# Attention backward: dK and dV products in bursts of two units instead of four, and operand loads cut into pieces on the queue of the crossbar transposes

## The chip, the core and the metric

The kernel runs on one core of one Trainium2 chip. The metric is the device time of one execution in microseconds. Three executions of the kernel before took 3423.2, 3423.9 and 3430.5 us; their median is 3423.9 us. One more execution was profiled: it took 3429.95 us, and its span from the first to the last instruction is 3427.8 us.

The engines are named as the profile names them: PE is the matrix engine (PEld its weight loads), DVE the vector engine, ACT the scalar engine with the exponential, POOL the GpSimd engine, SP the engine that issues most transfers. POOL and SP are used for transfers here: POOLq and SPq are the transfers that they issue.

## What is computed

The reference runs a transformer block with adaptive layer norms and takes its gradients for an output gradient. The change touches the backward pass of the attention alone: 32 heads of 16 columns over a sequence of 2048. Cut to that:

```python
q, k, v = (qkv[0], qkv[1], qkv[2])
scale = Dh ** (-0.5)
scores = jnp.einsum('bhqd,bhkd->bhqk', q, k) * scale
p = _softmax(scores, axis=-1)
o = jnp.einsum('bhqk,bhkd->bhqd', p, v)
...
_out, _vjp = jax.vjp(_f, A_x, A_wqkv, A_wo, B_w1, B_b1, B_w2, B_b2, c, w_mod)
_grads = _vjp(grad_out)
```

For each head the backward pass needs the probabilities again, the gradient of the scores from them and from dO times V, and then three products: dV from the probabilities and dO, dK from the score gradient and Q, dQ from the score gradient and K.

## The kernel before

The kernel is one program of several phases. The change lies in `attn_bwd`, which runs from about 1657 to 3251 us of the span.

**Tiling.** Heads go in quads `g` (8 of them), each in two pairs `jp` (16 pairs in all). For a pair the 2048 key columns go in 4 chunks `c` of 512, and for each chunk the 2048 query rows go in 16 tiles `ib` of 128. One pair of heads, one chunk and one row tile make a **unit** (1024 in all), and four units make a **group** (G = 4; 256 groups, 16 in a pair).

**One unit.** For each of its two heads `a`, PE computes a 128x512 tile of scores `st` (line 1198), ACT takes the exponential into one half of `pu` (line 1200), and PE computes a 128x512 tile of `dp`, dO times V (line 1201). The row sums that a softmax needs are folded into extra operand columns, so nothing else is done per element. Then DVE multiplies `dp` and `pu` into the unit's part of `ds` (line 1205). `st` has two buffers of one head, `dp` two of a unit: `dp` of a unit can't begin before DVE has read `dp` of the unit two before it, and `st` of a head can't begin before ACT has read `st` of the head two before it.

**dK and dV.** `kv` (line 1131) makes four products per unit, of 16 output rows by 512 columns each, into four bands of rows of one accumulator `acckv`, over the 16 row tiles of a chunk; the four run side by side on PE. They are collected in `pend` and run as **bursts**: `kv_group`, called after the second unit of a group, takes the four units of the group before it. After the last row tile of a chunk, DVE moves `acckv` into `kvT` (line 1134). After the last chunk of a pair, `turn` transposes `kvT` on PE in 16 steps (line 1140) into a buffer of `dp`, and ACT copies the result out (line 1144). `turn` runs ahead of the fourth unit of a group.

**dQ.** At the end of a group a crossbar transpose, issued by SP (line 1212), turns the 1 MB of `ds` into `dsT`. Its products `accq` (line 1151, eight per unit, 16 columns each) are laid between the matmuls of the units of the third group after it; DVE moves `accq` out once per pair (line 1158).

**Loads.** A quad needs `QT` and `dOT` (512 KB each) and `K`, `Q`, `dO` (256 KB each), in two buffers; `load_group` (lines 1117 and 1121) issues them on POOL at the start of the quad before. Each pair needs four masked operands, `KTm` and `VTm`, of 32 rows by 2048 columns; `load_masked` (line 462) issues them on POOL in pieces of 512 columns.

**Order.** PE runs in the order in which the code is written. The other engines' orders are made by a scheduler, within what the dependences allow. Each engine works through its own order strictly, so an instruction that waits holds up all behind it.

Of the kernel before, what the change touches and what calls it, by code (L numbers as in the profile page):

```python
# [8 lines left out]
BF16 = mybir.dt.bfloat16  # L9
# [9 lines left out]
P = 128  # L19
# [4 lines left out]
def chunks(total, size):  # L24
    out = []
    s = 0
    while s < total:
        w = min(size, total - s)
        out.append((s, w))
        s += w  # L30
    return out


class K:
# [219 lines left out]
    def phase12(self):  # L254
# [8 lines left out]
        with tc.tile_pool(name="p12", bufs=1) as sb, tc.tile_pool(name="p12e", bufs=8) as eb:  # L263
# [117 lines left out]
            with tc.tile_pool(name="p2c", bufs=1) as cp, tc.tile_pool(name="p2q", bufs=2) as qp, \  # L381
# [12 lines left out]
                for pidx in range(2 * NQ):  # L394
                    g, jp = divmod(pidx, 2)
                    heads = [4 * g + 2 * jp + a for a in range(2)]
                    if jp == 0:
                        T = self.load_quad(qp, srcs, g)
                    KT = T["KT"]
                    self.load_masked(masked, {"QT": (self.QTq_d, 0)}, g, jp)  # L400
# [679 lines left out]
    def attn_bwd(self):  # L1080
# [7 lines left out]
        tc, nc = self.tc, self.nc  # L1088
        S, D, H, NQ, ST, SC = self.S, self.D, self.H, self.NQ, self.ST, self.SC
        G = 4  # L1090
        W = 4 * DH
        with ExitStack() as es:
            qp = es.enter_context(tc.tile_pool(name="p5q", bufs=2))
            pup = es.enter_context(tc.tile_pool(name="p5pu", bufs=9))
            dsp = es.enter_context(tc.tile_pool(name="p5ds", bufs=3))
            dtp = es.enter_context(tc.tile_pool(name="p5dt", bufs=4))
            kvp = es.enter_context(tc.tile_pool(name="p5kv", bufs=1))
# [12 lines left out]
            masked = self.make_masked(cp, ["KT", "VT"])  # L1110
            pend, pendq = [], []

            def load_group(g):
                T = {}
                for n, src in fm.items():
                    t = qp.tile([P, S], BF16, name=f"{n}q")
                    nc.gpsimd.dma_start(t[:], src[g])
                    T[n] = t
                for n, src in tm.items():
                    t = qp.tile([P, ST, W], BF16, name=f"{n}g")  # L1120
                    nc.gpsimd.dma_start(t[:].rearrange("p st w -> p (st w)"), src[g])
                    T[n] = t
                return T

            def kv(u):
                (T, g, jp, c, ib, kvT, pu, ds) = u
                for j, (n, src) in enumerate((("Q", ds), ("dO", pu))):
                    for a in range(2):
                        r = 64 * j + 32 * a
                        col = (2 * jp + a) * DH  # L1130
                        nc.tensor.matmul(acckv[r:r + DH, :], lhsT=T[n][:, ib, col:col + DH], rhs=src[:, a, :],  # L1131
                                         start=(ib == 0), stop=(ib == ST - 1))
                if ib == ST - 1:
                    nc.vector.tensor_scalar(kvT[:, 512 * c:512 * (c + 1)], acckv[:], kvs[:], None, ALU.mult)

            def turn(g, jp, kvT):
                h0 = 4 * g + 2 * jp
                tp = dpp.tile([P, ST, P], BF16, name="dp")
                for st in range(ST):
                    nc.tensor.transpose(tp[:, st, :], kvT[:, st * P:(st + 1) * P], self.ident[:])  # L1140
                v = tp[:].rearrange("p s (t a e) -> p t s a e", t=2, a=2)
                for t, dst in enumerate((self.dk_t, self.dv_t)):
                    d = dst[:, :, h0 * DH:(h0 + 2) * DH].rearrange("p s (a d) -> p s a d", a=2)
                    nc.scalar.copy(d, v[:, t, :, :, 0:DH])

            def dq(u, heads):
                (T, g, jp, c, ib, i, dsT) = u
                for a in heads:
                    col = (2 * jp + a) * DH
                    for sub in range(4):  # L1150
                        nc.tensor.matmul(accq[:, ib, a, :], lhsT=dsT[:, (i * 2 + a) * 4 + sub, :],  # L1151
                                         rhs=T["K"][:, 4 * c + sub, col:col + DH],
                                         start=(c == 0 and ib == 0 and a == 0 and sub == 0), stop=False,
                                         skip_group_check=True)
                if c == SC - 1 and ib == ST - 1 and 1 in heads:
                    h0 = 4 * g + 2 * jp
                    d = self.dq_t[:, :, h0 * DH:(h0 + 2) * DH].rearrange("p s (a d) -> p s a d", a=2)
                    nc.vector.tensor_scalar(d, accq[:], self.scale, None, ALU.mult)

            def kv_group():  # L1160
                for u in pend[:G]:
                    kv(u)
                (T, g, jp, c, ib, kvT, pu, ds) = pend[G - 1]
                del pend[:G]
                return (g, jp, kvT) if c == SC - 1 and ib == ST - 1 else None

            msrc = {"KT": (self.KTq_d, 0), "VT": (self.VTq_d, 2)}
            self.load_masked(masked, msrc, 0, 0)
            T = load_group(0)
            turnq, hold = [], 0  # L1170
            with tc.manual_schedule(engines={mybir.EngineType.PE}):
                for g in range(NQ):
                    Tn = load_group(g + 1) if g + 1 < NQ else None
                    for jp in range(2):
                        if 2 * g + jp + 1 < 2 * NQ:
                            self.load_masked(masked, msrc, (2 * g + jp + 1) // 2, 1 - jp, eng=nc.gpsimd)
                        kvT = kvp.tile([P, S], BF16, name="kvT")
                        for c in range(SC):
                            c0 = 512 * c
                            for ib0 in range(0, ST, G):  # L1180
                                dsg = dsp.tile([P, G, 2, 512], BF16, name="ds")
                                for i in range(G):
                                    ib = ib0 + i
                                    q = slice(ib * P, (ib + 1) * P)
                                    uqs = []
                                    if len(pendq) > 2 * G:
                                        if pendq[0][3] == 0 and pendq[0][4] == 0 and hold:
                                            hold -= 1
                                        else:
                                            hold = 2 if pendq[0][4] else 0  # L1190
                                            uqs = [pendq.pop(0) for _ in range(2 if len(pendq) > 3 * G - i else 1)]
                                    if turnq and i == 3:
                                        turn(*turnq.pop(0))
                                    dp = dpp.tile([P, 2, 512], F32, name="dp")
                                    pu = pup.tile([P, 2, 512], BF16, name="pu")
                                    for a in range(2):
                                        stt = stp.tile([P, 512], F32, name="st")
                                        nc.tensor.matmul(stt[:], lhsT=T["QT"][:, q], rhs=masked["KT"][2 * jp + a][:, c0:c0 + 512],  # L1198
                                                         start=True, stop=True)
                                        nc.scalar.activation(pu[:, a, :], stt[:], ACT.Exp, scale=self.scale)  # L1200
                                        nc.tensor.matmul(dp[:, a, :], lhsT=T["dOT"][:, q], rhs=masked["VT"][2 * jp + a][:, c0:c0 + 512],  # L1201
                                                         start=True, stop=True)
                                        for uq in uqs:
                                            dq(uq, [a])
                                    nc.vector.tensor_tensor(dsg[:, i], dp[:], pu[:], ALU.mult)  # L1205
                                    pend.append((T, g, jp, c, ib, kvT, pu, dsg[:, i]))
                                    if i == 1 and len(pend) >= G + 2:
                                        r = kv_group()
                                        if r:
                                            turnq.append(r)  # L1210
                                dsT = dtp.tile([P, 8 * G, P], BF16, name="dsT")
                                nc.sync.dma_start_transpose(dsT[:], dsg[:].rearrange("p i a k -> p (i a k)"))
                                for i in range(G):
                                    pendq.append((T, g, jp, c, ib0 + i, i, dsT))
                    T = Tn
                turn(*kv_group())
                while pendq:
                    dq(pendq.pop(0), [0, 1])

# [263 lines left out]
```

## Time and profile before

| what | us |
|---|---|
| median of three executions | 3423.9 |
| the profiled execution | 3429.95 |
| its span | 3427.8 |
| PE busy in the span | 2957.0 (86%) |
| ACT busy | 2392.2 (70%) |
| DVE busy | 1877.4 (55%) |
| POOL busy | 372.7 (11%) |

The busy times are shares of a span with several phases, each with its own limit, so they don't tell what bounds the attention backward pass. PE busy counts pipelined matmuls by modelled ends: a PE that is shown as busy can still be waiting for its next operand. The DMA share counts the time of packets in flight on the core's 16 transfer engines; it goes over 1 where packets overlap. For a phase the useful views are the windows (busy time by stretch), the waits (who waited for whom) and the timeline (instructions in order, equal ones merged to a count, with the idle time before them and what ended it).

### The profile page before, as it was taken

The numbers are of one execution on the slowest core, as the hardware profiler recorded it, in microseconds if no ns is written. First come the engines' busy times: TensorE is split into PE (matmuls) and PEld (weight loads), VectorE is DVE, ScalarE is ACT, GpSimd is POOL, SyncE is SP. The second block draws the span as 40 slices with busy tenths as digits, with TensorE's granted clock in tenths as the row PEclk, the third lists the DMA queues.
The fourth block names the chain that finished last, engine by engine and source line by source line (L and its number), as shares of the span: only waits on it lengthen the run. The fifth ranks groups of instructions, "written<-read, shape, count | busy, mean of one in ns | idle before, by whom it ended". The sixth has DMA issues, their size and how long they took to land. (4 is left out here: it accounts for less than half of the span.)

```text
span 3427.8 us, 75641 instructions
## 1 busy us (share of the span) xinstructions
PE 2957.0 (86%) x31556; PEld 1444.9 (42%) x31556; DVE 1877.4 (55%) x2745; ACT 2392.2 (70%) x3577; POOL 372.7 (11%) x583
## 2 busy tenths in 40 slices
PE   5999998888884968578898998989999898999887
PEld 2455543333332433246444444444444444444433
DVE  6222220000004346545687887878788787888665
ACT  3899999999993324433576776777777777777633
POOL 3111210000002003330101010010101001000000
PEclk7999999999997989789999999999999999999998
DMA  3211110000004256564799999999999999999952
GB/s 116 68 50 49 45 46 11 6 12 12 6 1 153 96 175 216 118 204 140 156 181 184 182 188 182 180 189 179 192 183 187 186 178 194 179 179 176 188 172 66
DMA packets 1178339, 447.82 MB, mean 131 GB/s; under 512 B 1089162, under 2 KB 1145612, under 8 KB 1177996
## 3 DMA queue, kind: packets, MB, share of 16 engines
q1 hardware_dynamic: 1140188, 353.70, 53.4%
q0 software_dynamic: 29184, 79.59, 7.9%
q10 hardware_dynamic: 8624, 9.70, 0.9%
q8 instruction: 247, 4.05, 0.5%
q14 instruction: 96, 0.79, 0.1%
HBM read 106.83 MB, written 67.64 MB: 51 GB/s over the span
## 5 line engine op out<-in xcount | busy, mean ns | idle before, releaser
L1200 ACT ACTIVATE pu<-st 128x512 bf16<-128x512 f32 x2048 | 1143.5, 597 | 411.1 <-PE st L1198 404.3
L1205 DVE TENSOR_TENSOR ds<-dp,pu 128x1024 bf16<-128x1024 f32 x1024 | 1212.5, 1220 | 323.8 <-ACT pu L1200 306.4
L413 ACT ACTIVATE pu<-st 128x1024 bf16<-128x1024 f32 x1024 | 940.1, 1376 | 4.7 <-PE accbank L419 4.7
L1201 PE MATMUL dp<-VTm,dOTq 128*128 128x512 bf16 x2048 | 778.1, 380 | 102.9 <-DVE ds L1205 101.3
L1198 PE MATMUL st<-KTm,QTq 128*128 128x512 bf16 x2048 | 778.8, 380 | 8.2 <-DMA dOTq<-dOTq_d 7.6
L1151 PEld LDWEIGHTS <-dsT 128*128 128x128 bf16 x8192 | 488.4, 96 | 650.9 <-issue 203.1
L410 PE MATMUL st<-QTm,KTq 128*128 128x512 bf16 x2048 | 607.0, 377 | 7.0 <-ACT pu L413 1.5
L1151 PE MATMUL accq<-Kg,dsT 128*128 128x16 bf16 x8192 | 493.6, 170 | 33.0 <-DMA dsT<-ds 33.0
L419 PEld LDWEIGHTS <-pu 128*128 128x128 bf16 x8192 | 291.2, 96 | 458.7 <-ACT pu L413 408.2
L419 PE MATMUL accbank<-Vaug,pu 128*128 128x17 bf16 x8192 | 353.4, 172 | 67.6 <-DVE accbank L406 7.4
L428 DVE RECIPROCAL rl<-accbank 128x4 f32<-128x4 f32 x128 | 23.0, 180 | 526.0 <-PE accbank L419 525.6
L1131 PE MATMUL acckv<-ds,Qg 128*16 128x512 bf16 x2048 | 267.0, 382 | 0.8 <-DVE ds L1205 0.7
L1131 PE MATMUL acckv<-pu,dOg 128*16 128x512 bf16 x2048 | 267.0, 382 | 0.0
L1198 PEld LDWEIGHTS <-QTq 128*128 128x128 bf16 x2048 | 196.0, 96 | 134.5 <-issue 131.2
L1201 PEld LDWEIGHTS <-dOTq 128*128 128x128 bf16 x2048 | 196.8, 96 | 27.9 <-DVE ds L1205 18.7
L462 POOL DMA_DIRECT2D KTm<-KTq_d x120 | 60.0, 500 | 1121.3 <-PE dp L1201 1037.0
L288 DVE TENSOR_SCALAR ev_fm<-pps,bcol 128x512 bf16<-128x512 f32 x92 | 69.1, 751 | 195.5 <-PE pps L281 194.6
L410 PEld LDWEIGHTS <-KTq 128*128 128x128 bf16 x2048 | 129.6, 96 | 35.5 <-issue 20.5
L281 PE MATMUL pps<-xhat1T,wpad 128*128 128x512 bf16 x384 | 122.8, 378 | 4.9 <-DVE ev_fm L288 3.8
L1131 PEld LDWEIGHTS <-Qg 128*16 128x16 bf16 x2048 | 74.4, 88 | 74.7 <-issue 10.7
L549 ACT ACTIVATE rT<-ups,bias 128x512 bf16<-128x512 f32 x56 | 38.5, 688 | 52.1 <-PE ups L547 52.0
L1131 PEld LDWEIGHTS <-dOg 128*16 128x16 bf16 x2048 | 74.2, 88 | 0.0
(304 smaller groups left out, 2383.1 us busy)
## 6 DMA issues: line engine op xcount, KB each, us to landing
rT_d<-rT SPq DMA_DIRECT2D x4, 1792.0 KB
rT<-rT_d SPq DMA_DIRECT2D x4, 1792.0 KB
duT_d<-duT POOLq DMA_DIRECT2D x4, 1792.0 KB, 12.7
rT_f<-rT_d SPq DMA_DIRECT2D x14, 512.0 KB
duT_f<-duT_d POOLq DMA_DIRECT2D x14, 512.0 KB, 3.9
xhat_d<-xhat SPq DMA_DIRECT2D x2, 2048.0 KB
QTq_d<-ev_fm POOLq DMA_DIRECT2D x32, 128.0 KB, 2.1
QTm<-QTq_d SPq DMA_DIRECT2D x128, 32.0 KB
```

What stands on the lines that cost most here:

```text
L281: nc.tensor.matmul(pt[:, :sw], lhsT=wpads[t][:, kt, g, :], rhs=xhat1T[:, kt, s0:s0 + sw], start=(kt == 0), stop=(kt == DT - 1))
L288: nc.vector.tensor_scalar(ev[:, :sw], pt[:, :sw], bc, None, ALU.add)
L410: nc.tensor.matmul(stt[:, a, :qw], lhsT=KT[:, kb * P:(kb + 1) * P], rhs=QTm[a][:, q0:q0 + qw], start=True, stop=True)
L413: nc.scalar.activation(pu[:, :, :qw], stt[:, :, :qw], ACT.Exp, scale=self.scale)
L419: nc.tensor.matmul(acc[:, a, sub, :], lhsT=pu[:, a, sub * P:(sub + 1) * P], rhs=Vaug[:, kb, heads[a], :], start=False, stop=False, skip_gr ...
L462: eng.dma_start(masked[n][j][r:r + 32, c0:c0 + cw], src[g, r:r + 32, c0:c0 + cw])
L1131: nc.tensor.matmul(acckv[r:r + DH, :], lhsT=T[n][:, ib, col:col + DH], rhs=src[:, a, :], start=(ib == 0), stop=(ib == ST - 1))
L1151: nc.tensor.matmul(accq[:, ib, a, :], lhsT=dsT[:, (i * 2 + a) * 4 + sub, :], rhs=T["K"][:, 4 * c + sub, col:col + DH], start=(c == 0 and i ...
L1198: nc.tensor.matmul(stt[:], lhsT=T["QT"][:, q], rhs=masked["KT"][2 * jp + a][:, c0:c0 + 512], start=True, stop=True)
L1200: nc.scalar.activation(pu[:, a, :], stt[:], ACT.Exp, scale=self.scale)
L1201: nc.tensor.matmul(dp[:, a, :], lhsT=T["dOT"][:, q], rhs=masked["VT"][2 * jp + a][:, c0:c0 + 512], start=True, stop=True)
L1205: nc.vector.tensor_tensor(dsg[:, i], dp[:], pu[:], ALU.mult)
```

## The change

`kv_group` becomes `kv_two`: it runs two units and is called after the second and after the fourth unit of a group, whenever four units are pending. `turn` moves from ahead of the fourth unit to ahead of the third. `pu` gets 6 buffers instead of 9. `load_group` only makes a list of pieces: `QT` and `dOT` in two halves of 256 KB, `K`, `Q` and `dO` whole. `pair_pieces` lists the four masked operands of a pair in pieces of 32 rows by 2048 columns. The main loop issues one piece on SP ahead of a group, and all loads leave POOL.

```diff
-            pup = es.enter_context(tc.tile_pool(name="p5pu", bufs=9))
+            pup = es.enter_context(tc.tile_pool(name="p5pu", bufs=6))
...
             def load_group(g):
-                T = {}
+
+                T, pieces = {}, []
                 for n, src in fm.items():
-                    t = qp.tile([P, S], BF16, name=f"{n}q")
-                    nc.gpsimd.dma_start(t[:], src[g])
-                    T[n] = t
+                    t = T[n] = qp.tile([P, S], BF16, name=f"{n}q")
+                    for (s0, sw) in chunks(S, 1024):
+                        pieces.append((t[:, s0:s0 + sw], src[g, :, s0:s0 + sw]))
                 for n, src in tm.items():
-                    t = qp.tile([P, ST, W], BF16, name=f"{n}g")
-                    nc.gpsimd.dma_start(t[:].rearrange("p st w -> p (st w)"), src[g])
-                    T[n] = t
-                return T
+                    t = T[n] = qp.tile([P, ST, W], BF16, name=f"{n}g")
+                    pieces.append((t[:].rearrange("p st w -> p (st w)"), src[g]))
+                return T, pieces
+
+            def pair_pieces(g, jp):
+                pieces = []
+                for n, src, sh in (("KT", self.KTq_d, 0), ("VT", self.VTq_d, 2)):
+                    for j in (2 * jp, 2 * jp + 1):
+                        r = 32 * ((j + sh) % 4)
+                        pieces.append((masked[n][j][r:r + 32, :], src[g, r:r + 32, :]))
+                return pieces
...
-            def kv_group():
-                for u in pend[:G]:
+            def kv_two():
+                for u in pend[:2]:
                     kv(u)
-                (T, g, jp, c, ib, kvT, pu, ds) = pend[G - 1]
-                del pend[:G]
+                (T, g, jp, c, ib, kvT, pu, ds) = pend[1]
+                del pend[:2]
                 return (g, jp, kvT) if c == SC - 1 and ib == ST - 1 else None
...
-                    Tn = load_group(g + 1) if g + 1 < NQ else None
                     for jp in range(2):
-                        if 2 * g + jp + 1 < 2 * NQ:
-                            self.load_masked(masked, msrc, (2 * g + jp + 1) // 2, 1 - jp, eng=nc.gpsimd)
+                        pieces = []
+                        if jp == 0:
+                            pieces = pair_pieces(g, 1)
+                        elif g + 1 < NQ:
+                            Tn, pieces = load_group(g + 1)
+                            pieces = pair_pieces(g + 1, 0) + pieces
...
+                                if pieces and (c or ib0):
+                                    nc.sync.dma_start(*pieces.pop(0))
...
-                                    if turnq and i == 3:
+                                    if turnq and i == 2:
                                         turn(*turnq.pop(0))
...
-                                    if i == 1 and len(pend) >= G + 2:
-                                        r = kv_group()
+                                    if i % 2 == 1 and len(pend) >= 4:
+                                        r = kv_two()
```

**What PE runs around `turn`.** The first place is the start of the second pair of heads on PE. The rows are instructions in PE's order; `...` stands for rows that repeat these and for the dQ products. Before, the burst (here its last product) is followed by the two heads of the third unit, and only then come the transposes of `kvT` and the fourth unit:

```order
L1131 MATMUL acckv<-pu,dOg 16x512
L1198 LDWEIGHTS QTq
L1198 MATMUL st<-KTm_20941,QTq 128x512
...
L1201 MATMUL dp<-VTm_20949,dOTq 128x512
...
L1198 MATMUL st<-KTm_20943,QTq 128x512
...
L1140 LDWEIGHTS kvT
L1140 MATMUL dp<-ident,kvT 128x128
```

At the same place the change has, after the end of the burst, the transposes at once and then the third unit:

```order
L1139 MATMUL acckv<-pu,dOg 16x512
L1148 LDWEIGHTS kvT
L1148 MATMUL dp<-ident,kvT 128x128
...
L1211 LDWEIGHTS QTq
L1211 MATMUL st<-KTm_20941,QTq 128x512
...
L1214 MATMUL dp<-VTm_20949,dOTq 128x512
```

So the unit that stood between the burst and `turn` is gone from there. DVE's order of `ds` and `kvT` is the same before and after: the move of `acckv` stands behind the `ds` of the unit that precedes the burst.

**What SP runs around the start of a quad.** Before, SP has nothing but the 256 transposes in this phase. With the change its order around the start of the second quad is the following (`x15` counts equal rows; `KTm_20945` and `_20947` are the masked operands of the next pair but one half, `QTq` to `dOg` those of the quad after):

```order
L1225 DMA_TRANSPOSE dsT<-ds 128x32x128 x15
L1193 DMA KTm_20945<-KTq_d 32x2048
L1193 DMA KTm_20947<-KTq_d 32x2048
L1225 DMA_TRANSPOSE dsT<-ds 128x32x128
L1193 DMA VTm_20953<-VTq_d 32x2048
L1193 DMA VTm_20955<-VTq_d 32x2048
L1193 DMA QTq<-QTq_d 128x1024
L1225 DMA_TRANSPOSE dsT<-ds 128x32x128
L1193 DMA QTq<-QTq_d 128x1024
L1193 DMA dOTq<-dOTq_d 128x1024
L1225 DMA_TRANSPOSE dsT<-ds 128x32x128
L1193 DMA dOTq<-dOTq_d 128x1024
```

Behind these stand `Kg` and `Qg`, a transpose, `dOg`, and twelve transposes more. The scheduler has not kept one piece per group: eleven pieces stand among five transposes, up to three in a row, at the start of a quad; at the start of a quad's second pair four pieces stand around one transpose.

More of the change, by code (lines that the diff above doesn't have):

```diff
@@ L1158, in dq @@
                     nc.vector.tensor_scalar(d, accq[:], self.scale, None, ALU.mult)
-            def kv_group():
-                for u in pend[:G]:
+            def kv_two():
+                for u in pend[:2]:
                     kv(u)
-                (T, g, jp, c, ib, kvT, pu, ds) = pend[G - 1]
-                del pend[:G]
+                (T, g, jp, c, ib, kvT, pu, ds) = pend[1]
+                del pend[:2]
                 return (g, jp, kvT) if c == SC - 1 and ib == ST - 1 else None
-            msrc = {"KT": (self.KTq_d, 0), "VT": (self.VTq_d, 2)}
-            self.load_masked(masked, msrc, 0, 0)
-            T = load_group(0)
+            T, pieces = load_group(0)
+            for (d, sr) in pair_pieces(0, 0) + pieces:
+                nc.sync.dma_start(d, sr)
             turnq, hold = [], 0
@@ L1215, in attn_bwd @@
                     T = Tn
-                turn(*kv_group())
+                turn(*kv_two())
                 while pendq:
```

## The prediction

> **What bounds the kernel now.** I read the windows first, for the stretch in which the changed code runs, then the waits in it, then the timeline of one group. The columns of a window are its length, the busy time of PE, PEld, DVE, ACT and POOL with counts, the granted PE clock, the DMA share and GB/s.
>
> ```profile
> 1659.00:3240.00 1581.00, 1449.52 (x16556) 708.59 (x16556) 1262.98 (x1106) 1157.64 (x2079) 127.44 (x255) 0.99 1.04 183
> ```
>
> The phase takes 1581 us, 46% of the span. PE is busy for 92% of it, DVE for 80%, ACT for 73%: no engine is full, so the loop between them must set the pace. The waits of this stretch (who waited for whom, us in total, times, longest) say where:
>
> ```profile
> ACT pu L1200 <- PE st L1198: 404.3, 525, 7.7
> DVE ds L1205 <- ACT pu L1200: 306.4, 502, 7.5
> PE dp L1201 <- DVE ds L1205: 101.3, 271, 0.7
> PEld L1151 <- DMA dsT<-ds: 34.1, 7, 7.8
> ```
>
> ACT waits for PE, DVE for ACT and PE for DVE, some 500 times or two per group of 256: a ring. Apart from it, PE's weight loads waited 34.1 us for a late transpose, in 7 pieces of up to 7.8 us. The timeline of one group (start us, length, engine, line, count, idle time before) shows the ring turning:
>
> ```profile
> 2301.52 0.38 PE L1198 MATMUL st<-KTm,QTq 128*128 128x512 bf16 x1
> 2302.12 0.39 PE L1131 MATMUL acckv<-ds,Qg 128*16 128x512 bf16 x2
> 2302.78 0.38 PE L1131 MATMUL acckv<-ds,Qg 128*16 128x512 bf16 x2
> 2303.10 0.39 PE L1198 MATMUL st<-KTm,QTq 128*128 128x512 bf16 x1
> 2303.53 2.73 ACT L1200 ACTIVATE pu<-st 128x512 bf16<-128x512 f32 x5 [0.99 <-PE st L1198]
> 2303.64 0.38 PE L1198 MATMUL st<-KTm,QTq 128*128 128x512 bf16 x1
> 2304.69 2.36 DVE L1205 TENSOR_TENSOR ds<-dp,pu 128x1024 bf16<-128x1024 f32 x2 [0.90 <-ACT pu L1200]
> 2305.24 0.38 PE L1198 MATMUL st<-KTm,QTq 128*128 128x512 bf16 x1
> 2305.97 0.38 PE L1201 MATMUL dp<-VTm,dOTq 128*128 128x512 bf16 x1 [0.35 <-DVE ds L1205]
> 2306.28 0.38 PE L1198 MATMUL st<-KTm,QTq 128*128 128x512 bf16 x1
> 2306.81 0.38 PE L1198 MATMUL st<-KTm,QTq 128*128 128x512 bf16 x1
> 2307.09 0.38 PE L1201 MATMUL dp<-VTm,dOTq 128*128 128x512 bf16 x1
> 2307.41 0.38 PE L1198 MATMUL st<-KTm,QTq 128*128 128x512 bf16 x1
> 2308.02 0.39 PE L1131 MATMUL acckv<-ds,Qg 128*16 128x512 bf16 x2
> ```
>
> From burst to burst (2302.12 to 2308.02) a group takes 5.90 us. One head takes 0.535 us (2303.10 to 2303.64 and on to 2305.24, four heads), eight of them 4.28. The burst of four rounds holds PE from 2302.12 to 2303.10, 0.98 us, and begins 0.065 us later than a head would have (2301.52 + 0.535). Its rounds start 0.22 us apart (2302.12 to 2302.78 in three steps), so 0.88 is work and 0.165 its two edges. That makes 5.33; the other 0.57 is waiting: `st` at 2305.24 is followed at 2306.28 (1.04, so 0.505 too much) and 2306.81 at 2307.41 (0.065). During a burst nothing new reaches ACT, so DVE starts late afterwards (2304.69, after 0.90 idle), and the third unit behind the burst finds `dp` occupied.
>
> **The change, part by part.**
>
> *Two bursts of two units.* Each costs two rounds and two edges, 0.44 + 0.165 = 0.605 us; two of them and eight heads make 4.28 + 1.21 = 5.49. Does the wait go? Two units and a burst last 4 x 0.535 + 0.605 = 2.745 us. Counted from the first `st` behind a burst (2303.10), the next-but-one unit's `dp` would come at 2.745 + 0.22 (one matmul) = 2.965, one unit later 4.035. DVE released them at 2305.97 and 2307.09, 2.87 and 3.99 behind that `st`. Both are in time, by 0.095 and 0.045 us; DVE then has its next unit only 2.745 us after the last start, against 2 x 1.14 of work (2.36 for two in the row, whose last lasts 1.22). So the wait goes, narrowly: 5.90 - 5.49 = 0.41 per group, 256 x 0.41 = **105 us** gained. I take the margins as they stand; if they fail by 0.05 us it is 512 x 0.05 = 26 less.
>
> The Trainium skill, "TensorEngine Tiling (Array Packing)", section "Key Properties", says that a change of the tiling mode drains PE; it speaks against twice as many bursts, and the edges agree with it. By it the edges' 0.165 x 256 = 42 us is the price, which stands in the sum above already; without it the gain would be 147.
>
> *The move of `acckv` into `kvT`.* These rows are DVE's moves and ACT's copies:
>
> ```profile
> L1134 DVE TENSOR_SCALAR kvT<-acckv,kvs 128x512 bf16<-128x512 f32 x64 | 47.5, 742 | 0.5 <-PE acckv L1131 0.5
> L1158 DVE TENSOR_SCALAR dq_t<-accq 128x512 bf16<-128x512 f32 x15 | 10.2, 680 | 0.0
> ```
>
> Before, DVE's idle 0.90 us covered the 0.74. Afterwards DVE has 2.745 - 2.28 = 0.465 idle per two units, so each of the 48 moves that isn't ahead of a `turn` pushes DVE back by about 0.28, of which the margins take 0.1: 0.18 x 48 = **9 us** lost (bounds 0 and 48 x 0.74 = 36). The 15 moves of `accq` meet the same lack of cover: 16 x 0.2 = **3 us**.
>
> *`turn` directly behind the burst.* Before, around a `turn`:
>
> ```profile
> 2355.15 0.39 PE L1131 MATMUL acckv<-ds,Qg 128*16 128x512 bf16 x2
> 2356.12 0.39 PE L1198 MATMUL st<-KTm,QTq 128*128 128x512 bf16 x1
> 2356.73 0.74 DVE L1134 TENSOR_SCALAR kvT<-acckv,kvs 128x512 bf16<-128x512 f32 x1
> 2357.20 1.05 PE L1140 MATMUL dp<-ident,kvT 128*128 128x128 bf16 x16
> 2358.29 0.59 ACT L1144 COPY dk_t<-dp 128x512 bf16<-128x512 bf16 x1 [0.61 <-PE dp L1140]
> 2359.25 2.74 ACT L1200 ACTIVATE pu<-st 128x512 bf16<-128x512 f32 x5
> 2362.59 0.39 PE L1131 MATMUL acckv<-ds,Qg 128*16 128x512 bf16 x2
> ```
>
> That group took 7.44 us, 1.54 over a usual one: about the 1.05 of the transposes and a wait of half a microsecond. The unit between burst and `turn` (2356.12 to 2357.20) covered DVE's move. With the change nothing stands there. The `ds` ahead of the move ends 3.99 - 2.745 = 1.2 us after the burst, the move about 1.9, so the last four transposes wait and end near 2.25 (their first twelve read older chunks). ACT's two copies then hold it for 0.96 (2358.29 to 2359.25), so the third unit's first exponential starts near 3.4 instead of 2.25 + 0.43, and with two buffers of `st` the fourth unit waits the 0.7 out. So `turn` costs 2.25 + 0.7 = 2.95 in place of 1.54: 16 x 1.4 = **22 us** lost. Bounds: 0 if the copies find cover, 16 x 2.5 = 40 if both waits are felt in full twice.
>
> *Loads on SP.* SP's own instructions, and the two transposes around a load of quad operands beside a usual one:
>
> ```profile
> L1212 SPq DMA_TRANSPOSE dsT<-ds x256: 4766/5049/16257, 1665.1 to 3238.1; - x128
> L462 SPq DMA_DIRECT2D KTm<-KTq_d x8: 313/417/553, 1485.3 to 1489.9; - x8
> 2251.92 13.19 SPq L1212 DMA_TRANSPOSE dsT<-ds  x1
> 2301.18 4.79 SPq L1212 DMA_TRANSPOSE dsT<-ds  x1
> QTq<-QTq_d POOLq DMA_DIRECT2D x8, 512.0 KB, 5.1
> dOTq<-dOTq_d POOLq DMA_DIRECT2D x8, 512.0 KB, 6.6
> 2265.00:2271.00 6.00, 2.29 (x17) 1.03 (x18) 1.18 (x2) 1.19 (x2) 0.00 (x0) 0.82 1.24 215
> ```
>
> The transpose that meets POOL's load takes 13.19 us instead of 4.79, and soon after (2265 to 2271) PE is busy for 2.29 of 6 us at a clock of 0.82. This is where the 34.1 us of the waits come from. On SP the pieces stand in line with the transposes. For SP, a quad is 32 transposes of 5.05 (median) and 15 pieces of 0.42, 168 us, against at least 32 x 5.49 = 176 for PE: SP keeps up, by 5%. Locally, eleven pieces in five transposes add 4.6 us, while five groups leave 5 x (5.49 - 5.05) = 2.2 and the `turn` among them 2.95; and a transpose 8.4 us late cost a wait of at most 7.8, of 4.9 on average (34.1 / 7), so some 3.5 us of lateness aren't felt. I expect the load stalls to go but for **5 us**, a gain of 29; the bounds are 0 and 34 left. POOL's issues wait on nothing of the path, so their going gains nothing. Six buffers of `pu` cover four pending units and two in progress: no cost.
>
> *Sum*, against the profiled execution of 3429.95 us (its span 3427.8, about 2 us around it): 105 - 9 - 3 - 22 + 29 = 100 us gained, 3330. The profiled execution lies 6 us above the median of the three runs, so against that: 3423.9 - 100 = 3324 us.
>
> **The rivals.**
>
> *A: the load stall stays.* The same 2.25 MB must pass within five transposes; in line ahead of a transpose they delay it as they did beside it. For it: SP is left only 5%. Against it: the pieces are spread over some 28 us, where POOL issued all in about 5. All 34 stay: 3324 + 29 = 3353. The Trainium skill, "DMA: Bandwidth & Descriptors", section "Issuing engines are not separate DMA queues", would give this: transfers of all issuers run on the same engines, and the issuer changes only the time of issuing. No run here shows it for one queue yet.
>
> *B: the ring stays tight.* The margins of 0.095 and 0.045 us are small, and a burst of two rounds may have dearer edges than a quarter of a long one shows. At 0.05 per two units: 3324 + 26 = 3350.
>
> *C: the change doesn't do what it says.* DVE still holds PE up for the whole 0.57 per group, because a burst of any length empties ACT. Then the edges add 42, the moves and `turn` 34, the loads give 29: 47 us slower, 3471. Against it: the release times above.
>
> *D: ordinary transfers and transposes drain each other in one queue.* A quad has seven places where SP goes from transposes to pieces and back. If each costs D, SP needs 168 + 7D per quad. Today's pace is 1581 / 8 = 197.6 us, so it decides against the change from D = 4.2 us on; at the 6.6 us that a quad's `dOTq` took to land it is 214 per quad, 8 x 16.6 = 133 us slower, 3557 from the median. For it: landings of 5.1 and 6.6 us are of that size. Against it: POOL's pieces of `KTm` flowed beside transposes in every pair without lengthening a group.
>
> **Chances.** Forecast 0.62, A 0.16, B 0.14, C 0.03, D 0.05. The predicted time is that of the forecast. Its own range is 3308 (no load stall left, `turn` covered by half) to 3340; A and B reach to 3353 and, with each other in part, 3365. I give 3308 to 3365, which leaves out C, D and A with B in full. A measurement can tell about 0.2% (7 us) from no change: faster 0.91 (forecast, A, B less a remainder in which they add up), same 0.02, slower 0.07.
>
> **What the profile afterwards would show.** Right: bursts 2.75 us apart, the waits of `dp` for `ds` far under 101 us, PE busy near 98% between loads; after each pair one gap of 2 to 3 us with PE's transposes waiting for `kvT`; no transpose over 7 us, no PE wait for `dsT` over 2 us. A shows as waits for `dsT` of 4 to 8 us at the quads' starts; B as many waits of `dp` under 0.1 us; C as bursts 2.95 us apart; D as transposes or gaps of SP of 5 us and more around each piece. The forecast is wrong if two bursts and two pairs of units take more than 5.6 us, or if SP, never idle, sets the pace.

## The result, and the profile after

The changed kernel takes 3329.6 us (median of four runs, 3329.1 to 3331.1) against 3427.2 us (3423.2 to 3431.3) of the kernel before in the same runs: a ratio of 0.9716 [0.9699, 0.9733], faster. The profiled executions took 3329.45 and 3429.95 us: 100.5 us gained, and the account below is made between these two. Between the medians it is 97.7 us, and 3329.6 lies 5.6 us above the forecast of 3324, which was worked out from 3423.9 us before.

The windows view of the changed kernel over the stretch of the attention backward pass (columns as in the prediction):

```profile
1656.00:3150.00 1494.00, 1450.57 (x16611) 702.85 (x16609) 1257.00 (x1113) 1149.57 (x2083) 1.50 (x2) 1.00 1.08 196
```

The two windows leave out the ends of the phase, so their lengths aren't the gain: from its first `st` to its last move of `accq` the phase lasts 1500.2 us, and 1595.1 before. The PE work in it is the same: PE is now busy for 97% of the window, not 92%. POOL's 127 us of work have gone. The waits of this stretch, for the changed kernel (who waited for whom, us in total, times, longest):

```profile
ACT pu L1213 <- PE st L1211: 298.1, 527, 2.1
DVE ds L1218 <- ACT pu L1213: 226.9, 451, 5.0
...
PEld L1148 <- DVE kvT L1142: 17.3, 16, 1.1
...
PE dp L1148 <- DVE kvT L1142: 14.4, 15, 1.0
PEld L1159 <- DMA dsT<-ds: 13.6, 12, 2.4
...
PE accq L1159 <- DMA dsT<-ds: 7.7, 8, 1.9
PE dp L1214 <- DVE ds L1218: 5.8, 15, 0.4
```

The third link of the ring is open: `dp` waited 101.3 us in 271 pieces for `ds`, and now 5.8 us in 15. ACT and DVE still wait for what is ahead of them, but PE hardly waits for `ds` any more. Two larger waits of PE are left: sixteen times for `kvT`, once per pair, which is new, and twelve times for a transpose, 13.6 us instead of 34.1. Its timeline over one group (start us, length, engine, line, count, idle time before):

```profile
2300.25 0.39 PE L1139 MATMUL acckv<-ds,Qg 128*16 128x512 bf16 x2
2300.47 0.38 PE L1139 MATMUL acckv<-ds,Qg 128*16 128x512 bf16 x2
2300.80 0.39 PE L1211 MATMUL st<-KTm,QTq 128*128 128x512 bf16 x1
...
2301.34 0.38 PE L1211 MATMUL st<-KTm,QTq 128*128 128x512 bf16 x1
...
2302.38 2.35 DVE L1218 TENSOR_TENSOR ds<-dp,pu 128x1024 bf16<-128x1024 f32 x2 [0.40 <-ACT pu L1213]
...
2303.01 0.39 PE L1139 MATMUL acckv<-ds,Qg 128*16 128x512 bf16 x2
...
2305.77 0.39 PE L1139 MATMUL acckv<-ds,Qg 128*16 128x512 bf16 x2
```

The bursts start at 2300.25, 2303.01 and 2305.77: 2.76 us for two units, 5.52 for a group, in place of 5.90. Heads follow each other after 0.54 us and no `dp` waits. DVE idles 0.40 us per two units.

The timeline around a `turn` of the changed kernel:

```profile
2212.57 0.39 PE L1139 MATMUL acckv<-ds,Qg 128*16 128x512 bf16 x2
...
2213.22 0.83 PE L1148 MATMUL dp<-ident,kvT 128*128 128x128 bf16 x12
...
2214.21 0.74 DVE L1142 TENSOR_SCALAR kvT<-acckv,kvs 128x512 bf16<-128x512 f32 x1
...
2215.01 0.40 PE L1148 MATMUL dp<-ident,kvT 128*128 128x128 bf16 x4 [0.96 <-DVE kvT L1142]
...
2215.45 0.58 ACT L1152 COPY dk_t<-dp 128x512 bf16<-128x512 bf16 x1 [2.47 <-PE dp L1148]
...
2216.40 2.21 ACT L1213 ACTIVATE pu<-st 128x512 bf16<-128x512 f32 x4
...
2217.07 0.38 PE L1211 MATMUL st<-KTm,QTq 128*128 128x512 bf16 x1 [0.61 <-ACT pu L1213]
...
2218.21 0.39 PE L1139 MATMUL acckv<-ds,Qg 128*16 128x512 bf16 x2
```

From burst to burst 5.64 us instead of 2.76: a `turn` costs 2.88 us. Twelve transposes read older chunks; the last four wait 0.96 us for DVE's move, and a later `st` waits 0.61 us for ACT, which the copies had held.

Last, SP's own timeline at the start of a quad, and its transposes as a group (number: shortest, median, longest in ns), both of the changed kernel:

```profile
1838.61 5.18 SPq L1225 DMA_TRANSPOSE dsT<-ds  x1
1843.83 1.04 SPq L1193 DMA_DIRECT2D VTm<-VTq_d  x2
1844.92 1.33 SPq L1193 DMA_DIRECT2D QTq<-QTq_d  x1
1846.36 5.30 SPq L1225 DMA_TRANSPOSE dsT<-ds  x1
1851.70 0.57 SPq L1193 DMA_DIRECT2D QTq<-QTq_d  x1
1852.32 0.43 SPq L1193 DMA_DIRECT2D dOTq<-dOTq_d  x1
1852.85 5.87 SPq L1225 DMA_TRANSPOSE dsT<-ds  x1
1858.76 0.57 SPq L1193 DMA_DIRECT2D dOTq<-dOTq_d  x1
```

```profile
L1225 SPq DMA_TRANSPOSE dsT<-ds x256: 4699/5106/6867, 1662.8 to 3141.0; - x128
```

The longest transpose is 6.9 us, where those beside POOL's loads of a quad had taken 12 to 16. The scheduler lays one to three pieces between two transposes, not one as the code is written. For a while SP falls behind PE: from 1838.61 to the transpose at 1846.36 it takes 7.75 us, and PE's group 5.52.

### The profile page after: what moved, and what is told of

It reads as the page before. It is cut to its first block, busy times and chain, and to the rows that moved or that the text cites. A ratio compares the mean times of both kernels' runs of the same rounds, so it can differ in the third digit from the quotient of the medians.

```text
span 3327.6 us, 75207 instructions
## 1 busy us (share of the span) xinstructions
PE 2954.7 (89%) x31556; PEld 1438.8 (43%) x31556; DVE 1866.0 (56%) x2745; ACT 2381.2 (72%) x3577; POOL 231.7 (7%) x303
## 5 line engine op out<-in xcount | busy, mean ns | idle before, releaser
L1139 PE MATMUL acckv<-ds,Qg 128*16 128x512 bf16 x2048 | 309.1, 382 | 0.8 <-DVE ds L1218 0.7
L1139 PE MATMUL acckv<-pu,dOg 128*16 128x512 bf16 x2048 | 309.1, 382 | 0.0
L652 PE MATMUL daps<-gT,W2gbT 128*128 128x512 bf16 x224 | 58.5, 404 | 19.3 <-DVE duT L654 19.3
L725 ACT COPY a_blk<-trps 128x1024 bf16<-128x1024 bf16 x28 | 28.3, 1012 | 59.0 <-PE trps L722 58.9
```

Source lines behind the costliest of these rows:

```text
L652: nc.tensor.matmul(pt[:, :sw], lhsT=W2gbT[:, kt, ft * P:(ft + 1) * P], rhs=gT[:, kt, s0:s0 + sw], start=(kt == 0), stop=(kt == DT - 1))
```

## The experiments

Each kernel is the changed one with the edit shown (cut to its main lines), timed beside the kernel before on the chip that it ran on (about 3433 us there); ratios are to that.

**One part of the change at a time.** First, bursts of two, but the loads back on POOL, whole and at the places that they had before:

```diff
-    nc.sync.dma_start(*pieces.pop(0))
+    Tn = load_group(g + 1) if g + 1 < NQ else None
...
+    self.load_masked(masked, msrc, (2 * g + jp + 1) // 2, 1 - jp, eng=nc.gpsimd)
```

> The change's bursts, place of turn and buffers of pu, with the loads as before on POOL. Theory (the loads on SP gave back 26 us): the load stalls of about 38 us return, the time is 3330 + 26 = 3356 us, one transpose per quad takes 12 us or more, and groups stay at 5.52 us. Rival (the longer turn would have covered the loads anyway, the move to SP gains nothing): 3330 us, no load stall over 2 us.

Measured: 3358.9 us, ratio 0.978 [0.9765, 0.9794]. Groups take 5.52 us and the `turn` group 8.40 as in the change, and the stalls of before are back, as its waits and its group of transposes show:

```profile
PEld L1151 <- DMA dsT<-ds: 29.7, 13, 8.1
```

```profile
L1212 SPq DMA_TRANSPOSE dsT<-ds x256: 4768/5092/18602, 1667.2 to 3166.5; - x128
```

So the bursts with their `turn` are worth some 75 us alone (3433.3 - 3358.9), and the loads in pieces bring the rest, 22 us by the two ratios (0.978 - 0.9716, of 3433). Second, the other half alone:

```diff
-    pup = es.enter_context(tc.tile_pool(name="p5pu", bufs=6))
+    pup = es.enter_context(tc.tile_pool(name="p5pu", bufs=9))
...
-    if i % 2 == 1 and len(pend) >= 4:
-        r = kv_two()
+    if i == 1 and len(pend) >= G + 2:
+        r = kv_group()
...
-    if turnq and i == 2:
+    if turnq and i == 3:
```

> The change's loads on SP alone: bursts of four, turn ahead of the fourth unit and 9 buffers of pu as before. Theory (loads and bursts are separate gains): groups stay at 5.89 us, and since SP has more time per group than with short bursts, nearly all of the 38 us goes: 3427 - 35 = 3392 us. Rival (pieces in the queue of the transposes hold these up by themselves): stalls of dsT stay over 20 us in sum and the time is 3410 us or more.

Measured: 3399.8 us, 0.9893 [0.9876, 0.9911], 34 us gained by the times and groups of 5.89. The size is the expected one, but the stalls did not go nearly whole: the waits of PE's weight loads for `dsT` are 18.0 us in 8 pieces, half of the 34.1 before. This view shows only half of the gain. The lengths show more of it: the groups beside the loads lost some 38 us before and lose 13 here, and the phase is 25 us shorter (1569.7 us, 1595.1 before), of the 28 us between the two profiled executions (3429.95 and 3401.58). That these loads still stall PE, at a pace that leaves SP more time than in the change, was the first sign that SP's 5% of room isn't the whole matter.

**The place of `turn`.** One number moved back:

```diff
-    if turnq and i == 2:
+    if turnq and i == 3:
```

> The change with turn ahead of the fourth unit, as before, instead of the third. Theory (PE waits in turn because nothing stands between the burst and the transposes of kvT while DVE makes it): the unit in between covers DVE, turn costs 1.9 us instead of 2.88 over a usual group, 16 x 1.0 = 16 us less: 3314 us. Rival (ACT's copies and the buffer of dp that turn takes cost the same there): 3330 us, with the waits of PE for kvT replaced by waits of dp for ds or of st for pu.

Measured: 3320.1 us, 0.967 [0.9654, 0.9686]; a repetition beside other kernels:

> The change with turn ahead of the fourth unit once more, on the same chip as the run with the pieces in both pairs: ratio 0.967 if the two differ by their loads alone, and 14 to 20 us of waits of PE for dsT.

gave 3321.7 us, 0.9673 [0.9652, 0.9694]. The timeline of this kernel around the same `turn`:

```profile
2210.01 0.74 DVE L1142 TENSOR_SCALAR kvT<-acckv,kvs 128x512 bf16<-128x512 f32 x1
2210.15 1.06 PE L1148 MATMUL dp<-ident,kvT 128*128 128x128 bf16 x16
...
2211.94 0.38 PE L1214 MATMUL dp<-VTm,dOTq 128*128 128x512 bf16 x1 [0.51 <-DVE ds L1218]
```

One unit stands between burst and `turn` and covers DVE's move, so the sixteen transposes run in one go. The bursts around it start at 2208.37 and 2212.86, 4.49 us apart: `turn` costs 1.73 us here. Sixteen times 1.15 is 18 us; some 15 arrive (ratios 0.967 and 0.9673 against 0.9716, of 3433). The rest is given back in the waits for transposes, which rise from 13.6 us to 21.9, and to 24.9 in the repetition, where 14 to 20 were expected. I take it that SP had used the long pause of `turn` to catch up; no run shows this by itself:

```profile
PEld L1159 <- DMA dsT<-ds: 21.9, 14, 2.6
```

**What the loads still cost, and why.** If the clusters of pieces make the transposes late, an even spread should cure it. SP too in the order of the code, one piece per group:

```diff
-    with tc.manual_schedule(engines={mybir.EngineType.PE}):
+    with tc.manual_schedule(engines={mybir.EngineType.PE, mybir.EngineType.SP}):
```

> The change with SP's order as written in the code, so that one piece at most stands ahead of a transpose. Theory (the 12 us of load stall that are left come from two and three pieces in a row, at the quad's start, where SP is latest): no wait for dsT over 1 us, 3330 - 11 = 3319 us. Rival (SP and the transfer engines have no room for the bytes at this pace, however they are spread): stalls of 8 us or more in sum stay, only at other groups, and the time is 3325 to 3335 us.

Measured: 3342.7 us, 0.973 [0.9712, 0.9748], no better than the change. The theory fell, and the stalls of the rival came, at other groups: from about the tenth group of a quad's second pair on. Its waits and SP's timeline show why:

```profile
PEld L1159 <- DMA dsT<-ds: 34.4, 31, 3.0
```

```profile
2355.90 5.79 SPq L1225 DMA_TRANSPOSE dsT<-ds  x1
2361.74 0.57 SPq L1193 DMA_DIRECT2D dOTq<-dOTq_d  x1
2362.40 5.57 SPq L1225 DMA_TRANSPOSE dsT<-ds  x1
2368.03 0.57 SPq L1193 DMA_DIRECT2D dOTq<-dOTq_d  x1
2368.70 5.67 SPq L1225 DMA_TRANSPOSE dsT<-ds  x1
```

In these rows transposes take 5.6 to 5.8 us, with 0.7 us between them for a piece and its edges (2361.69 to 2362.40). From transpose to transpose that is 6.5 and 6.3 us, without a pause of SP, for what PE does in 5.52. These transposes are long ones: over all 49 behind a piece of 256 KB the median is 5.45 us (4.82 to 6.24), where the kernel without loads (below) has 5.06 at the same places. Behind a piece of 128 KB it is 5.14 against 4.90. The scheduler's clusters stood at the start of the quad, where `turn` (2.88 us) and the move of `accq` give SP time; the even spread takes its pieces out of that time. That this place is the reason is argued; no run put the clusters anywhere else.

Is it SP's issue time, or the transfers themselves? The same even spread, issued by ACT, which had room:

```diff
-    nc.sync.dma_start(*pieces.pop(0))
+    nc.scalar.dma_start(*pieces.pop(0))
...
-    with tc.manual_schedule(engines={mybir.EngineType.PE}):
+    with tc.manual_schedule(engines={mybir.EngineType.PE, mybir.EngineType.Activation}):
```

> The pieces spread as in the run with SP in code order, one ahead of a group, but issued by ACT (in code order too) and not by SP. Theory (SP's own time for a piece and the transpose behind it is what is short, not the transfer engines): with the pieces off SP nearly no wait for dsT is left, 12 us less than the change as a ratio of before: 0.968, and ACT, which is idle about 0.6 us per two units, hides the issues. Rival 1 (the transfer engines are short): the stalls of 15 to 20 us stay as in that run, ratio 0.973. Rival 2 (a piece on ACT delays the exponentials by its issue): groups with a piece last 0.3 us longer, 15 of 32, 8 x 15 x 0.3 = 36 us, ratio 0.978.

Measured: 3355.0 us, 0.9772 [0.9754, 0.979], worse than the change and than the same spread on SP. The ratio is that of rival 2, but its mechanism isn't there: in a quad's first pair and in the first seven groups of its second, groups with a piece are as long as in the change (5.52 us for most), so ACT's issuing is hidden. The transposes of this kernel as a group:

```profile
L1225 SPq DMA_TRANSPOSE dsT<-ds x256: 4685/5200/10882, 1663.2 to 3157.9; - x128
```

With SP free of issuing, the transposes beside pieces of 256 KB are longer still, 5.70 us in the median and up to 10.9, and PE's weight loads wait 33.1 us for transposes, about the 34.4 of the spread on SP, as rival 1 had it. So what is short isn't SP's own time for a piece, as the theory had it: what SP saves, the transposes beside the transfers take up. The profile leaves out a part: its execution is the fastest of the four (3347.1 to 3362.1 us), and that of the spread on SP the slowest of its four (3334.3 to 3345.8). What makes the others longer with ACT as the issuer wasn't seen. The same with `turn` later:

```diff
-    nc.sync.dma_start(*pieces.pop(0))
+    nc.scalar.dma_start(*pieces.pop(0))
...
-    with tc.manual_schedule(engines={mybir.EngineType.PE}):
+    with tc.manual_schedule(engines={mybir.EngineType.PE, mybir.EngineType.Activation}):
...
-    if turnq and i == 2:
+    if turnq and i == 3:
```

> The same with turn ahead of the fourth unit. Theory: both gains add, 12 us from the stalls and 18 us from turn, whose group lasts 7.25 us: ratio 0.963, the fastest of all. Rival (turn's shorter group takes away time in which late transposes catch up, as with turn alone): only part of the 12 us is had, ratio 0.966.

Measured: 3332.6 us, 0.9712 [0.9697, 0.9726], some 12 us slower than the later `turn` with SP's pieces, and outside both expectations. The later `turn` has its gain here too (3355.0 to 3332.6 us), but nothing came of the stalls: the waits for `dsT` are 35.9 us, without the one for the last transpose of the phase (41.3 with it).

How much is there to be had at all? The pieces of the loop left out:

```diff
-    pieces = pair_pieces(g, 1)
-elif g + 1 < NQ:
-    Tn, pieces = load_group(g + 1)
-    pieces = pair_pieces(g + 1, 0) + pieces
+    pieces = pair_pieces(g, 1) if g == 0 else []
+Tn = T
```

> The change with the pieces of the loop left out: the operands of the first quad are used for all quads, so the gradients of the others are not computed. Theory (the loads cost what the waits for dsT show, 12 us, and nothing else): no wait for dsT but the last, groups as before, 3330 - 12 = 3318 us as a ratio of 0.968. Rival (loads slow the groups in other ways, or the transposes are late on their own): stalls of dsT stay above 5 us or the ratio is under 0.965.

Measured: 3318.0 us, 0.9666 [0.9649, 0.9682]. Its transposes, and its only wait of PE's weight loads for `dsT`, which is that for the last transpose of the phase:

```profile
L1223 SPq DMA_TRANSPOSE dsT<-ds x256: 4666/4920/5617, 1664.9 to 3130.9; - x128
```

```profile
PEld L1159 <- DMA dsT<-ds: 5.1, 1, 5.1
```

All loads of the loop together cost the change 17 us (0.9716 - 0.9666, of 3433), near the 13.6 us that PE's waits show; the intervals leave some 8 us either way. Without them the median transpose is 4.92 us.

**The size of the burst.** Bursts of one unit:

```diff
-    for u in pend[:2]:
-        kv(u)
+    kv(pend[0])
...
-    if i % 2 == 1 and len(pend) >= 4:
+    if len(pend) >= 3:
```

> The change with a burst after every unit. Theory (a burst's two edges cost 0.165 to 0.18 us whatever its length, and no wait for DVE is left): a group lasts 4.28 + 4 x (0.22 + 0.18) = 5.88 us, 256 x 0.36 = 92 us more than the change, about 3425 us. Rival (a short burst has cheaper edges, or PE's edges lie beside waits that go): under 5.65 us, within 35 us of the change. Rival 2 (one round can't hide its four weight loads): over 6.1 us per group, 3480 us or more.

Measured: 3446.1 us, 1.0037 [1.0024, 1.0051], slower than before. The bursts in its timeline:

```profile
2299.90 0.39 PE L1139 MATMUL acckv<-ds,Qg 128*16 128x512 bf16 x2
...
2301.37 0.39 PE L1139 MATMUL acckv<-ds,Qg 128*16 128x512 bf16 x2
...
2302.85 0.39 PE L1139 MATMUL acckv<-ds,Qg 128*16 128x512 bf16 x2
```

A unit takes 1.475 us (2299.90 to 2302.85 for two): two heads are 1.07, the round 0.22, so the edges of a burst are 0.185 us, about as much as those of a burst of four. Four of them per group eat the gain: it is 5.90 us again (4 x 1.475). The expected time left out a wait that its records show, of PE's products for DVE's move of `acckv`, at the starts of chunks: 39.6 us in 48 pieces, since the next burst comes a unit earlier.

**The buffers of `pu`.**

```diff
-    pup = es.enter_context(tc.tile_pool(name="p5pu", bufs=6))
+    pup = es.enter_context(tc.tile_pool(name="p5pu", bufs=9))
```

> The change with nine buffers of pu as before. Theory (six cover four pending units and two in progress): no difference, ratio 0.9716 within its interval, groups 5.52 us. Rival (ACT is held up by the buffers of pu): faster by 5 us or more.

Measured: 3334.0 us, 0.9718 [0.9703, 0.9733], the ratio of the change. No cost of six buffers shows.

**The loads in both pairs.** `turn` later, SP in the order of the code, and the halves of `QT` and `dOT` moved to the pair before, so that the two pairs of a quad carry 8 and 7 pieces and not 4 and 11:

```diff
-    pieces = pair_pieces(g, 1)
+    pieces, rest = pair_pieces(g, 1), []
+    if g + 1 < NQ:
+        Tn, group = load_group(g + 1)
+        pieces, rest = pieces + group[:4], group[4:]
 elif g + 1 < NQ:
-    Tn, pieces = load_group(g + 1)
-    pieces = pair_pieces(g + 1, 0) + pieces
+    pieces = pair_pieces(g + 1, 0) + rest
...
-    with tc.manual_schedule(engines={mybir.EngineType.PE}):
+    with tc.manual_schedule(engines={mybir.EngineType.PE, mybir.EngineType.SP}):
...
-    if turnq and i == 2:
+    if turnq and i == 3:
```

> The change with turn ahead of the fourth unit, SP in code order, one piece ahead of a group, and the eleven pieces of a quad's second pair split: the two halves of QT and of dOT go into the first pair, K, Q and dO stay in the second. Theory (a piece makes the transposes beside it later by some 0.4 us against PE's pace, whoever issues it, and lateness of about 3.5 us isn't felt, so seven or eight pieces after each turn are hidden where eleven in one pair are not): waits of PE for dsT under 5 us in sum, ratio 0.962. Rival (any piece costs its time, however spread): 15 us or more of these waits stay, ratio 0.967 as with turn alone.

Measured: 3314.2 us, 0.9656 [0.9639, 0.9673], the fastest of all, though its interval overlaps that of the later `turn` alone. The waits for transposes did not fall under 5 us as expected:

```profile
PEld L1159 <- DMA dsT<-ds: 28.5, 30, 5.1
```

5.1 of this is the wait for the phase's last transpose. The other 23.4 us, in 29 short waits, are no less than the 21.9 and 24.9 of the later `turn` alone, as the rival had it. By the lengths of the groups the loads cost less, 14 us against 20 and 24, and beside the repetition on the same chip the time is 7 us shorter; with overlapping intervals this gain is likely, not shown.

## Why the prediction was right, step by step

The forecast was 100 us gained between profiled executions, and 100.5 came. The terms, measured from the starts of each group's first `st` in the two traces:

| step | predicted | measured | how |
|---|---|---|---|
| ring: no wait of `dp` | +105 | +97 | 256 x (5.90 - 5.52) |
| moves of `acckv` into `kvT` | -9 | -5 | 48 groups of 5.62, not 5.52 |
| moves of `accq` | -3 | -2 | 16 groups, 0.12 dearer than before |
| `turn` behind the burst | -22 | -21 | 16 x (2.88 - 1.54) |
| load stalls | +29 | +26 | lost in longer groups: 37.8, now 11.6 |
| phase starts earlier | none | +3 | first `st` at 1653.5, not 1656.6 |
| sum | +100 | +98 | |

The first five rows make 95 us, and the phase is 94.9 us shorter.

**The ring.** The step "the wait goes, narrowly" held with margins of 0.095 and 0.045 us. Rival C (the wait stays) would show 2.95 us between bursts; it is 2.76. The term was too large by 8 us: 2.76 where 2.745 was worked out. Rival B (dearer edges, a tighter ring) thus held for 0.015 us per two units, not for 0.05. The prediction says that PE, too, waited for DVE some 500 times; its row says 271, about once per group. The working went by the timeline, so nothing hangs on it. The edges are paid per burst, whatever its length: 0.165 us for four rounds, 0.18 for two (2.76 - 2.14 - 0.44), 0.185 for one.

**`turn`.** Mechanism and size came as worked out (2.95 predicted, 2.88 measured), and the later `turn` shows that it is a loss inside the change: some 15 us are had by leaving `turn` where it was.

**The loads.** The mechanism was right: cut into pieces in the line of transposes, they no longer make one transpose of 12 to 16 us. The size was off. I expected 5 us of stalls left and no wait over 2 us, and PE's waits show 13.6, the longest 2.4. The failing step is "a quad is 32 transposes of 5.05 and 15 pieces of 0.42": in the SP rows above a piece is 0.43 to 1.33 us, and a transpose beside pieces 5.2 to 5.9. Over all transposes behind a piece of 256 KB the mean is 5.56 us in the change, and 4.98 at the same places without loads. The 5% of room that was counted for SP isn't there while loads run. By the groups' lengths the gain is 26 us all the same, and 22 by the kernel with POOL's loads.

Rival A (the stall stays whole) fell, but its reasoning held in part: the same bytes must pass, and they still cost 17 us, as the kernel without loads shows. The rule of the Trainium skill that stood beside it, "DMA: Bandwidth & Descriptors", section "Issuing engines are not separate DMA queues", agrees with the profile of the pieces issued by ACT: another issuer left long transposes (5.70 us in the median, 5.45 on SP) and the waits of 33.1 us that the same spread had on SP (34.4). What part of the gain is due to cutting and spreading, and what to the queue, the runs don't tell apart: no run has whole loads on SP, and pieces on ACT came to 0.9772, not clearly better than whole loads on POOL (0.978), while the same spread on SP came to 0.973.

Rival D (each change between transposes and pieces drains the queue) fell: the gaps on SP between pieces and transposes are about 0.1 us (1852.75 to 1852.85, for one).

**The sum.** That it came within 1 us is partly luck: the ring gave 8 us less and the loads 3 less than reckoned; smaller losses of the moves and `turn` (6 in all), an earlier start (3) and a shorter stretch behind the phase (2: 173.9 us, 176.2 before) made up for it. How much of the earlier start is chance isn't known: the first `st` comes between 1650.4 and 1656.4 us in the kernels with SP's loads, and at 1656.6 and 1658.0 in the two with POOL's.

**Open.** What in the transfer engines makes a transpose longer beside ordinary transfers wasn't settled. Nor was why the pieces issued by ACT cost 12 us more by the medians than the same spread on SP, when the profiled executions of the two are alike.

## What to carry to other kernels

Where a ring of three engines turns on two buffers, work on one of them that gives the others nothing to do belongs in pieces small enough to pass before the next buffer is due, and no smaller, because each piece pays its edges again: here bursts of two units gained, and bursts of one lost all of it. Whatever had been hidden in the old pause (a move, a copy, a `turn`) must be placed anew, a unit after the one it depends on. Cutting a big load removes its one long stall, but its bytes can still lengthen the transfers beside it, as here; count the queue's time with the durations it has while the load runs, and try the load where the compute pauses anyway.

## What was not expected of the hardware

A crossbar transpose of 1 MB takes 4.92 us in the median with no other transfer in the loop (4.67 to 5.62). Behind a piece of 256 KB on SP it takes 5.45 us in the median where the same places without loads have 5.06, beside such pieces issued by ACT 5.70 and up to 10.9, and up to 18.6 beside whole loads from POOL.

Clusters of pieces at a place where PE pauses cost less (13.6 us of waits) than an even spread (34.4) in the profiled executions; the ratios of the two, 0.9716 and 0.973, overlap in their intervals.

And margins of 0.045 us in the ring were kept over a whole phase: the view shows 15 waits of `dp` for `ds`, 5.8 us in all, and each of the 15 comes some 2 us behind a move of `accq`, like this one:

```profile
2229.76 0.68 DVE L1166 TENSOR_SCALAR dq_t<-accq 128x512 bf16<-128x512 f32 x1
...
2231.63 0.39 PE L1214 MATMUL dp<-VTm,dOTq 128*128 128x512 bf16 x1 [0.39 <-DVE ds L1218]
```
